# Retention states padded with zeros to all 128 rows, and scores taken two blocks in a row

## The chip, the cores and the metric

The kernel runs on one core of one Trainium2 chip. The metric is the device time of one execution in microseconds (us), 614.69 us before the change as the median of three runs. The chip's engines are named as the profile names them: PE (the matrix engine; PEld is its weight load), DVE (VectorE), ACT (ScalarE), POOL (GpSimd) and SP (SyncE, which here only issues transfers).

## The reference

Retention (a linear attention with a decaying state) over 2 sequences of 768 tokens and 8 heads of 64, and behind it two gated layers on the 1536 tokens. Cut to what matters:

```python
for t in range(S):                                   # S = 768, D = 64, 8 heads, 2 sequences
    state = gamma * state + k[t] v[t]^T              # per head, 64 x 64
    y[t] = scale * q[t] @ state
x = y as (1536 tokens, 512)
x = (x @ w_a) * (x @ w_b) @ w_out                    # 512 -> 1536 -> 512
h = x @ w_in;  out = (h * sigmoid(1.702 h)) @ w_out2 # 512 -> 2048 -> 512
```

## The kernel before

The 1536 tokens are 12 blocks of 128 (`NBLK`), 6 for each sequence (`SEQ`). The retention of block n is worked out in chunks, with all decays moved into scaled copies of q and v, so that the running state is a plain sum in PSUM:

- `att_load(n)` fetches a block in two transfers of 512 KB each on SP's queue: `qv` (q transposed, and v) and `kk` (k transposed, and k). Four buffers of each exist (`RAWBUFS`), so the load of block n+4 waits until block n's have been read: `qv` by `att_q(n)` and `att_v(n)`, `kk` by `att_scores(n)` and `att_kv(n)`. SP issues in program order, so a load that waits holds back all that follow it.
- `att_q(n)` and `att_v(n)` are one POOL instruction each, the scaled q and v of a block.
- `att_scores(n)` (below "sc n"): 8 products k q^T on PE, two heads side by side in the array: head 0 of a pair in rows 0 to 63, head 1 in rows 64 to 127. Then DVE multiplies the 1024 columns by the causal mask (tile `a`). Scores of odd and even blocks have a PSUM tile each.
- `att_kv(n)` ("kv n"): 8 products k^T v, 64 x 64 per head, added to the state in PSUM; ACT copies the state to SBUF. The last block of a sequence needs none.
- `att_av(n)` ("av n" and, except in the first block of a sequence, "st n"): 8 products v^T a and 8 products state^T q into the same PSUM tile. The state products take 64 rows of one head against 64 rows of q, again two heads side by side. ACT and DVE then split the result into a high and a low part, `xh` and `xl`.

Each of these is an fp32 product, for which the profile holds two records: 8 products are x16. All instructions stand in program order by hand (a manual schedule): the loop over n at the end of the kernel writes, for n > 0, sc n+1, then q n+2 and v n+1, kv n, the early work on weights, av n and st n, and the load of block n+4. So PE's order is sc n+1, kv n, av n, st n, sc n+2, and so on.

In between, three 512 KB pieces of the first layer's weights are split into a high and a low part (`w_carry` on ACT; `w_bits`, `w_sign` and `w_add` on DVE, one step per block; `w_parts` on ACT and POOL, tile `wl`), and some more are loaded (`w_dma`, tile `wraw`, on SP's queue too). Behind the loop, `layer(1)` and `layer(2)` are long rows of 128x512 products on PE (`up`, `down`) with the other engines beside them.

Of the kernel before, what the change touches and what calls it, by code (L numbers as in the profile page):

```python
# [7 lines left out]
F32 = mybir.dt.float32  # L8
# [7 lines left out]
P = 128  # L16
B, H, S, D = 2, 8, 768, 64
NP = H // 2
# [6 lines left out]
SEQ = S // P  # L25
# [15 lines left out]
def retention_moe_kernel(  # L41
# [9 lines left out]
    nc = tc.nc  # L51
# [9 lines left out]
    attp = retention.enter_context(tc.tile_pool(name="attp", bufs=2))  # L61
    ps_att = retention.enter_context(tc.tile_pool(name="ps_att", bufs=1, space=PSUM))

    def lo_part(engine, lo, src, hi):
        engine.tensor_tensor(out=lo, in0=src, in1=hi.bitcast(F32), op=ALU.subtract)  # L65
# [8 lines left out]
    gdec = attp.tile([P, SEQ, NP], F32, tag="gdec", name="gdec", bufs=1)  # L74
    qdec = attp.tile([P, SEQ, NP, P], F32, tag="qdec", name="qdec", bufs=1)
    zero = attp.tile([P, P], F32, tag="zero", name="zero", bufs=1)
    x = [xp.tile([P, KD, NT], F32R, tag=t, name=t) for t in ("xh", "xl")]
    qv_t, kk_t, q_t, v_t, a_t, state_t = {}, {}, {}, {}, {}, {}
    kv_t = [None]

    def att_load(n):
        if n >= NBLK:
            return
        qv, kk = (attp.tile([P, 2, DM], F32, tag=t, name=t, bufs=RAWBUFS) for t in ("qv", "kk"))
        if n == 0:
            nc.sync.dma_start(out=qv[:, 0, :], in_=att[n][:, 0, :])
            nc.scalar.dma_start(out=kk[:, 0, :], in_=att[n][:, 1, :])
            nc.scalar.dma_start(out=causal[:, 0, :], in_=cmask[:, 0:P])
            nc.scalar.dma_start(
                out=vdec[:, 0].rearrange("p h o -> p (h o)"), in_=cdec[:, NP * P:NP * P + H]  # L90
            )
            nc.sync.dma_start(out=qv[:, 1, :], in_=att[n][:, 3, :])
            nc.sync.dma_start(out=kk[:, 1, :], in_=att[n][:, 2, :])
            nc.scalar.dma_start(out=qdec[:, 1].rearrange("p a t -> p (a t)"), in_=cdec[:, 0:NP * P])
        else:
            nc.sync.dma_start(out=qv, in_=att[n][:, 0:4:3, :])
            nc.sync.dma_start(out=kk, in_=att[n][:, 1:3, :])  # L97
        qv_t[n], kk_t[n] = qv, kk

    def att_constants():  # L100

        gamma = [1.0 - 2.0 ** (-5.0 - h) for h in range(H)]
        for c in range(1, SEQ):
            for h in range(H):
                nc.gpsimd.memset(vinv[:, c, h, :], gamma[h] ** (-float(P) * c))
        for c in (2, 0, 3, 4, 5):
            for h in range(H):
                rows = slice(64 * (h % 2), 64 * (h % 2) + 64)
                nc.gpsimd.memset(gdec[rows, c, h // 2:h // 2 + 1], gamma[h] ** (float(P) * (c - 1)))
# [6 lines left out]
    def att_qdec(c):  # L116

        if c < SEQ and c != 1:
            for p in range(NP):
                nc.scalar.activation(  # L120
                    out=qdec[:, c, p], in_=qdec[:, 1, p], func=ACTF.Copy, scale=gdec[:, c, p:p + 1]
                )

    def att_q(n):
        if n < NBLK:
            t = attp.tile([P, NP, P], F32, tag="q", name="q", bufs=4)
            (nc.vector if n == 1 else nc.gpsimd).tensor_tensor(  # L127
                out=t, in0=qv_t[n][:, 0, :].rearrange("p (a t) -> p a t", t=P), in1=qdec[:, n % SEQ], op=ALU.mult
            )
            q_t[n] = t  # L130
# [12 lines left out]
    def att_scores(n):  # L143

        if n >= NBLK:
            return
        if n % 2:
            ps = ps_att.tile([P, 2, G], F32, tag="sc", name="ps_sc")
        else:
            ps = ps_a.tile([P, NG, G], F32, tag="set", name="ps_sc")  # L150

        q = qv_t[n][:, 0, :].rearrange("p (a t) -> p a t", t=P) if n == 0 else q_t[n]
        for p in range(NP):
            for h2 in range(2):
                rows = slice(64 * h2, 64 * h2 + 64)
                nc.tensor.matmul(  # L156
                    ps[:, h2, p * P:(p + 1) * P],
                    kk_t[n][rows, 0, p * P:(p + 1) * P],
                    q[rows, p, :],
                    start=True,  # L160
                    stop=True,
                )
        a = attp.tile([P, 2 * NP, P], F32, tag="a", name="a")
        nc.vector.tensor_tensor(
            out=a,
            in0=ps[:, 0:2, :].rearrange("p c (a t) -> p (c a) t", t=P),
            in1=causal.to_broadcast([P, 2 * NP, P]),
            op=ALU.mult,
        )
        a_t[n] = a  # L170

    def att_kv(n):
        c = n % SEQ
        if c == SEQ - 1:
            return
        if c == 0:
            kv_t[0] = ps_att.tile([P, NP, D], F32, tag="kv", name="ps_kv")
        ps = kv_t[0]

        for p in range(NP):  # L180
            for h2 in range(2):
                h = 2 * p + h2
                nc.tensor.matmul(  # L183
                    ps[64 * h2:64 * h2 + 64, p, :],
                    kk_t[n][:, 1, h * D:(h + 1) * D],
                    v_t[n][:, h, :],
                    start=(c == 0 and p == 0),
                    stop=True,
                    skip_group_check=True,
                )  # L190
        t = attp.tile([P, NP, D], F32, tag="state", name="state")
        nc.scalar.copy(t, ps)
        state_t[n + 1] = t

    def att_av(n):
        c = n % SEQ
        ps = ps_att.tile([P, NP, P], F32, tag="av", name="ps_av", bufs=2)
        for p in range(NP):
            for h2 in range(2):
                h = 2 * p + h2  # L200
                nc.tensor.matmul(  # L201
                    ps[64 * h2:64 * h2 + 64, p, :],
                    v_t[n][:, h, :],
                    a_t[n][:, NP * h2 + p, :],
                    start=(p == 0),
                    stop=(c == 0),
                    skip_group_check=True,
                )
        if c > 0:
            for p in range(NP):  # L210
                for h2 in range(2):
                    rows = slice(64 * h2, 64 * h2 + 64)
                    nc.tensor.matmul(  # L213
                        ps[rows, p, :],
                        state_t[n][rows, p, :],
                        q_t[n][rows, p, :],
                        start=False,
                        stop=True,
                        skip_group_check=True,
                    )  # L220
        hi, lo = (t[:, :, n * P:(n + 1) * P] for t in x)
        if n == 0:
            t = attp.tile([P, NP, P], F32, tag="q", name="x0", bufs=4)
            nc.vector.tensor_tensor(out=t, in0=ps, in1=qdec[:, 0], op=ALU.mult)
            ps = t
        nc.scalar.copy(hi, ps)
        lo_part(nc.vector, lo, ps, hi)
# [229 lines left out]
    def warm(ps, n):  # L457

        for _ in range(n):
            nc.tensor.matmul(ps[:, 0, :], zero, zero, start=True, stop=True)  # L460

    with tc.manual_schedule():
        nc.vector.memset(zero, 0.0)
        att_constants()
        for n in range(RAWBUFS):
            att_load(n)
        ps = ps_att.tile([P, NP, P], F32, tag="av", name="ps_warm", bufs=2)
        warm(ps, WARM)
        att_v(0)
        att_vdec([1])  # L470
        nc.vector.tensor_scalar(
            out=causal, in0=causal, scalar1=0.0, scalar2=1.0, op0=ALU.is_gt, op1=ALU.mult
        )
        att_scores(0)
        att_q(1)
        att_qdec(2)
        warm(ps, 12)
        for n in range(NBLK):
            if n > 0:
                att_scores(n + 1)  # L480
            if n == 0:
                att_v(1)
                att_q(2)
                att_vdec(range(2, SEQ))
            else:
                att_q(n + 2)
                att_v(n + 1)
            att_kv(n)
            if n == 0:
                att_qdec(0)  # L490
            if n + 3 < SEQ:
                att_qdec(n + 3)
            w_early(n)
            att_av(n)
            if n == 0:
                att_scores(1)
            if n + RAWBUFS < NBLK:
                att_load(n + RAWBUFS)
            if n in (0, 1, 2, 9):
                w_dma()  # L500
            if n % 3 == 1 and n // 3 < EARLY:
                w_carry(n // 3)
        layer(1)
        layer(2)
# [66 lines left out]
```

## Time and profile before

| what | value |
|---|---|
| runs | 614.69 us median of 3 (614.07 to 614.81) |
| profiled execution | 614.94 us, of which the span from first to last instruction is 613.2 us |
| PE busy | 604.5 us, 99% of the span |
| PEld, DVE, ACT, POOL busy | 502.8, 374.6, 236.9, 149.9 us |
| chain that ended last | PE 97%, of it L340 (`up`) 53% and L377 (`down`) 37% |
| first product of `layer(1)` on that chain | 52.98 us after the span's start |

The retention lies in the first 53 us; the two layers take the rest. A busy PE is not a PE at its peak: between products of different shapes it can stand still inside what the profile calls busy.

### The profile page before, as it was taken

The page shows a single profiled execution, that of the slowest core. Times are in us where ns is not written, and L with a number is a line of the kernel's source. Part 1 is how long each engine was busy: PE and PEld are TensorE (multiplying, and loading weights), DVE is VectorE, ACT ScalarE, POOL GpSimd, SP SyncE. Part 2 cuts the span into 40 slices and gives each one's busy share as a digit, 9 for nine tenths or more (in the row PEclk, how much of TensorE's full clock was granted, in tenths as well). Part 3 has the DMA queues.
Part 4 walks back from the last instruction along what each step waited for, and adds up shares of the span by engine and source line. Part 5 has one row for each costly group of instructions (what it writes and reads, how often), then busy time and mean ns, then how long its engine had stood idle before and what let it go on. Part 6 is the DMA issues. An engine that isn't in the chain of part 4 may idle for free.

```text
span 613.2 us, 7880 instructions
## 1 busy us (share of the span) xinstructions
PE 604.5 (99%) x3198; PEld 502.8 (82%) x3198; DVE 374.6 (61%) x414; ACT 236.9 (39%) x340; POOL 149.9 (24%) x179
## 2 busy tenths in 40 slices
PE   7999999999999999999999999999999999999996
PEld 7888888888888888888888888888888888888885
DVE  1694487882258874156778578825786387826422
ACT  3451455362145530134452365624543155403400
POOL 6692132232023311012332113211212022302000
PEclk9999999999999999999999999999999999999999
DMA  8991133332122322011332011321223111200022
GB/s 304 397 352 38 36 103 104 103 106 66 35 65 73 104 69 69 0 44 60 104 103 81 23 49 54 103 70 35 68 69 103 35 46 57 69 0 1 0 104 103
DMA packets 17043, 52.21 MB, mean 85 GB/s; under 512 B 1776, under 2 KB 1904, under 8 KB 17008
## 3 DMA queue, kind: packets, MB, share of 16 engines
q1 hardware_dynamic: 16432, 51.12, 25.1%
q10 hardware_dynamic: 576, 0.59, 0.3%
q8 instruction: 25, 0.41, 0.3%
q14 instruction: 10, 0.08, 0.0%
HBM read 48.57 MB, written 3.15 MB: 84 GB/s over the span
## 4 chain that ended last, share of the span: by engine, by line
PE 97%; DMA 2%; DVE 0%; POOL 0%; DVEq 0%; SPq 0%; issue 0%; POOLq 0%
PE ps L340 53%; PE ps L377 37%; PE ps_sc L156 2%; PE ps_av L201 2%; PE ps_av L213 2%; DMA qv<-in_att_dram 1%; PE ps_kv L183 1%; DMA kk<-in_att_dram 1%; DVE part L394 0%; POOL q L127 0%; DVEq L567 0%; SPq L97 0%; POOLq L127 0%
## 5 line engine op out<-in xcount | busy, mean ns | idle before, releaser
L65 POOL TENSOR_TENSOR wl<-wt,wh 128x512 fp32r<-128x512 f32 x68 | 116.7, 1719 | 405.7 <-ACT wh L285 375.8
L340 PE MATMUL ps<-xh,wh 128*128 128x512 f32 x480 | 128.9, 389 | 0.0
L340 PE MATMUL ps<-xh,wl 128*128 128x512 f32 x480 | 128.8, 389 | 0.0
L340 PE MATMUL ps<-xl,wh 128*128 128x512 f32 x480 | 128.8, 389 | 0.0
L340 PEld LDWEIGHTS ps<-xh,wl 128*128 128x128 f32 x480 | 90.1, 188 | 18.7
L340 PEld LDWEIGHTS ps<-xh,wh 128*128 128x128 f32 x480 | 90.0, 188 | 18.8 <-issue 0.2
L340 PEld LDWEIGHTS ps<-xl,wh 128*128 128x128 f32 x480 | 90.1, 188 | 18.7
L266 DVE TENSOR_SCALAR wt<-wt 128x512 f32<-128x512 f32 x68 | 65.3, 960 | 53.5 <-ACT wt L260 53.5
L357 ACT CAST gh<-sb 128x1536 fp32r<-128x1536 f32 (+1 forms) x42 | 44.2, 1051 | 112.6 <-DVE sb L356 106.3
L356 DVE TENSOR_TENSOR sb<-ps,sb 128x1536 f32<-128x1536 f32 (+1 forms) x42 | 51.2, 1220 | 48.8 <-ACT sb L440 24.5
L65 DVE TENSOR_TENSOR gl<-sb,gh 128x1536 fp32r<-128x1536 f32 (+1 forms) x42 | 51.5, 1226 | 47.1 <-ACT gh L357 47.1
L394 DVE TENSOR_TENSOR part<-ps,part 128x1536 f32<-128x1536 f32 (+1 forms) x24 | 35.5, 1487 | 48.2 <-PE ps L377 48.2
L273 DVE SCALAR_TENSOR_TENSOR wt<-wraw,wt 128x512 int32<-128x512 int32 x68 | 57.5, 846 | 2.2
L285 ACT CAST wh<-wt 128x512 fp32r<-128x512 f32 x68 | 41.9, 616 | 39.7 <-DVE wt L279 39.7
L377 PE MATMUL ps<-wl,gh 128*128 128x512 f32 x192 | 55.2, 389 | 0.0
L377 PE MATMUL ps<-wh,gh 128*128 128x512 f32 x192 | 55.2, 389 | 0.0
L377 PE MATMUL ps<-wh,gl 128*128 128x512 f32 x192 | 55.2, 389 | 0.0
L279 DVE CUSTOM_DVE_ANT_0 wt<-wraw,wt 128x1024 uint16<-128x1024 uint16 x68 | 50.0, 736 | 6.4
L260 ACT ACTIVATE wt<-wraw 128x512 f32<-128x512 f32 x68 | 45.7, 672 | 1.9 <-POOL wl L65 1.5
L261 ACT ACTIVATE wraw<-wraw 128x512 int32<-128x512 uint32 x68 | 45.3, 667 | 0.0
L440 ACT ACTIVATE sb<-ps 128x1536 f32<-128x1536 f32 (+1 forms) x24 | 23.8, 1029 | 54.1 <-PE ps L340 54.0
L434 ACT COPY sb<-ps 128x1536 f32<-128x1536 f32 x12 | 17.3, 1444 | 66.4 <-PE ps L340 66.4
(47 smaller groups left out, 556.1 us busy)
## 6 DMA issues: line engine op xcount, KB each, us to landing
wraw<-in_w_dram SPq DMA_DIRECT2D x68, 512.0 KB, 3.7
qv<-in_att_dram SPq DMA_DIRECT2D x11, 512.0 KB, 8.3
kk<-in_att_dram SPq DMA_DIRECT2D x11, 512.0 KB, 7.3
out_dram<-part SPq DMA_DIRECT2D x3, 768.0 KB, 3.5
out_dram<-part SPq DMA_DIRECT2D x3, 256.0 KB, 2.1
qv<-in_att_dram SPq DMA_DIRECT2D x2, 256.0 KB, 4.6
kk<-in_att_dram ACTq DMA_DIRECT2D x1, 256.0 KB, 4.2
kk<-in_att_dram SPq DMA_DIRECT2D x1, 256.0 KB, 5.9
```

The costliest lines, as they stand in the source:

```text
L65: engine.tensor_tensor(out=lo, in0=src, in1=hi.bitcast(F32), op=ALU.subtract)
L260: nc.scalar.activation(out=wt[i], in_=high.bitcast(F32), func=ACTF.Abs)
L261: nc.scalar.activation(out=low, in_=low.bitcast(U32), func=ACTF.Copy, scale=2.0 ** -29)
L266: nc.vector.tensor_scalar(out=t, in0=t, scalar1=F64_LOW, scalar2=F64_HIGH, op0=ALU.max, op1=ALU.min)
L273: nc.vector.scalar_tensor_tensor(out=ti, in0=wraw[i][:, :, 1], scalar=-0x40000000, in1=ti, op0=ALU.bitwise_and, op1=ALU.bitwise_or)
L279: nc.vector.tensor_tensor(out=ti, in0=ti, in1=wraw.pop(i)[:, :, 0], op=ALU.add)
L285: nc.scalar.copy(hi, t)
L340: nc.tensor.matmul(ps[:, g, :], l, r, start=(i == 0 and k == 0), stop=(i == 2 and k == max(late or now)), skip_group_check=True,)
L356: nc.vector.tensor_tensor(out=sb[:, c], in0=ps[:, c], in1=sb[:, c], op=ALU.mult)
L357: nc.scalar.copy(gh[:, c], sb[:, c])
L377: nc.tensor.matmul(ps[:, n, :], l, r, start=(f == min(g_t) and i == 0), stop=(f == max(g_t) and i == 2), skip_group_check=True,)
L394: nc.vector.tensor_tensor(out=t[:, c], in0=ps[:, c], in1=t[:, c], op=ALU.add)
```

## The change

Three things change. First, the state gets two fixed tiles of 128 x 4 x 2 x 64, zeroed once on DVE at the start. ACT copies each head's half of the state into its own place, so that the other head's 64 rows stay zero: two copies of 64 partitions each instead of one of 128. Second, the state products take all 128 rows of that tile and of q: the zero rows add nothing, and the product has the shape of the one before it (128 rows, 64 columns). Third, from block 4 on the scores of two blocks stand in a row: at n = 3, 5, 7 and 9 the loop writes sc n+1 and sc n+2, at even n none. For that q is made a block earlier (`att_q(n + 3)` from n = 2 on), q has five buffers and `a` three, and the decays of q are scaled a block earlier.

```diff
+    state = [attp.tile([P, NP, 2, D], F32, tag=f"state{i}", name=f"state{i}", bufs=1) for i in range(2)]
...
-            t = attp.tile([P, NP, P], F32, tag="q", name="q", bufs=4)
+            t = attp.tile([P, NP, P], F32, tag="q", name="q", bufs=5)
...
-        a = attp.tile([P, 2 * NP, P], F32, tag="a", name="a")
+        a = attp.tile([P, 2 * NP, P], F32, tag="a", name="a", bufs=3)
...
-        t = attp.tile([P, NP, D], F32, tag="state", name="state")
-        nc.scalar.copy(t, ps)
-        state_t[n + 1] = t
+        for h2 in range(2):
+            rows = slice(64 * h2, 64 * h2 + 64)
+            nc.scalar.copy(state[(n + 1) % 2][rows, :, h2, :], ps[rows])
...
-                    rows = slice(64 * h2, 64 * h2 + 64)
                     nc.tensor.matmul(
-                        ps[rows, p, :],
-                        state_t[n][rows, p, :],
-                        q_t[n][rows, p, :],
+                        ps[64 * h2:64 * h2 + 64, p, :],
+                        state[n % 2][:, p, h2, :],
+                        q_t[n][:, p, :],
...
         nc.vector.memset(zero, 0.0)
+        for t in state:
+            nc.vector.memset(t, 0.0)
...
         for n in range(NBLK):
-            if n > 0:
+            if n in (1, 2):
                 att_scores(n + 1)
+            elif n % 2:
+                att_scores(n + 1)
+                att_scores(n + 2)
             if n == 0:
                 att_v(1)
                 att_q(2)
                 att_vdec(range(2, SEQ))
             else:
-                att_q(n + 2)
+                if n < 3:
+                    att_q(n + 2)
+                if n > 1:
+                    att_q(n + 3)
                 att_v(n + 1)
             att_kv(n)
             if n == 0:
                 att_qdec(0)
-            if n + 3 < SEQ:
-                att_qdec(n + 3)
+            for c in ((3,), (4, 5))[n] if n < 2 else ():
+                att_qdec(c)
```

On PE, the last stretch of the retention before the change. The names are the program's: q_660 and kk_592 are block 10's, q_710 and kk_643 block 11's; v_662 is block 9's.

```order
L156 MATMUL ps_sc_699<-q_660,kk_592 128x128 x8
L183 MATMUL ps_kv_568<-v_662,kk_550 64x64 x8
L201 MATMUL ps_av_725<-a_658,v_662 64x128 x8
L213 MATMUL ps_av_725<-q_606,state_672 64x128 x8
L156 MATMUL ps_sc_746<-q_710,kk_643 128x128 x8
L183 MATMUL ps_kv_568<-v_712,kk_592 64x64 x8
L201 MATMUL ps_av_772<-a_708,v_712 64x128 x8
L213 MATMUL ps_av_772<-q_660,state_722 64x128 x8
L201 MATMUL ps_av_795<-a_755,v_757 64x128 x8
L213 MATMUL ps_av_795<-q_710,state_767 64x128 x8
```

So sc 11, the last to need loaded data, is followed by kv 10, av 10, st 10, av 11 and st 11. The same stretch after the change, where q_623 and kk_598 are block 10's, q_666 and kk_660 block 11's, and v_668 block 9's:

```order
L158 MATMUL ps_sc_705<-q_623,kk_598 128x128 x8
L158 MATMUL ps_sc_716<-q_666,kk_660 128x128 x8
L185 MATMUL ps_kv_574<-v_668,kk_567 64x64 x8
L203 MATMUL ps_av_740<-a_621,v_668 64x128 x8
L214 MATMUL ps_av_740<-q_570,state1_86 64x128 x8
L185 MATMUL ps_kv_574<-v_727,kk_598 64x64 x8
L203 MATMUL ps_av_776<-a_714,v_727 64x128 x8
L214 MATMUL ps_av_776<-q_623,state0_85 64x128 x8
L203 MATMUL ps_av_799<-a_725,v_761 64x128 x8
L214 MATMUL ps_av_799<-q_666,state1_86 64x128 x8
```

Now kv 9, av 9 and st 9 stand behind sc 11 as well.

On POOL, from q 8 to the last v before the change (q_564 is q 8, v_566 is v 7, then upward by one; wl is the low part of a weight piece):

```order
L127 TENSOR_TENSOR q_564<-qv_502,qdec_83 128x512
L135 TENSOR_TENSOR v_566<-qv_451,vdec_80 128x512
L127 TENSOR_TENSOR q_606<-qv_549,qdec_83 128x512
L135 TENSOR_TENSOR v_608<-qv_502,vdec_80 128x512
L127 TENSOR_TENSOR q_660<-qv_591,qdec_83 128x512
L135 TENSOR_TENSOR v_662<-qv_549,vdec_80 128x512
L65 TENSOR_TENSOR wl_675<-wt_506,wh_674 128x512
L127 TENSOR_TENSOR q_710<-qv_642,qdec_83 128x512
```

And after it, where q_537 is q 8, v_539 v 6, q_570 q 9, and so on:

```order
L129 TENSOR_TENSOR q_537<-qv_508,qdec_83 128x512
L137 TENSOR_TENSOR v_539<-qv_406,vdec_80 128x512
L65 TENSOR_TENSOR wl_542<-wt_355,wh_541 128x512
L129 TENSOR_TENSOR q_570<-qv_566,qdec_83 128x512
L137 TENSOR_TENSOR v_572<-qv_468,vdec_80 128x512
L129 TENSOR_TENSOR q_623<-qv_597,qdec_83 128x512
L137 TENSOR_TENSOR v_625<-qv_508,vdec_80 128x512
L129 TENSOR_TENSOR q_666<-qv_659,qdec_83 128x512
L137 TENSOR_TENSOR v_668<-qv_566,vdec_80 128x512
```

Before, v n stood behind q n+1; now it stands behind q n+2. The order of SP's transfers is the same in both.

## Rows read from the trace of the kernel before

**Rows 1.** Busy time in stretches: PE, PEld, DVE, ACT, POOL, PEclk, DMA share, GB/s.

```profile
20.00:25.00 5.00, 5.00 (x93) 4.41 (x94) 3.34 (x6) 3.80 (x9) 2.75 (x3) 1.00 1.02 390
40.00:45.00 5.00, 5.00 (x92) 4.36 (x90) 4.97 (x6) 3.24 (x6) 4.62 (x5) 1.00 0.99 346
```

**Rows 2.** Chain that ended last, in order of time: start, us, what.

```profile
14.60 1.95 PE ps_sc L156 x16
...
28.27 0.61 PE ps_kv L183 x16
28.89 0.88 PE ps_av L201 x16
...
31.88 1.02 PE ps_av L201 x16
...
46.31 1.02 PE ps_av L213 x16
47.34 1.09 PE ps_sc L156 x16
...
52.98 22.23 PE ps L340 x97
```

**Rows 3.** Groups by line and shape, PEld, 18.2 to 52.9 us.

```profile
L201 PEld LDWEIGHTS ps_av<-a,v 128*64 128x64 f32 x170 | 9.2, 138 | 0.3 <-issue 0.2
L213 PEld LDWEIGHTS ps_av<-q,state 64*64 64x64 f32 x160 | 8.5, 133 | 1.7 <-issue 1.7
```

**Rows 4.** Timeline of SP's queue, issues of loads: start us, us.

```profile
22.62 0.38 SPq L96 DMA_DIRECT2D qv<-in_att_dram  x1
...
26.22 0.38 SPq L96 DMA_DIRECT2D qv<-in_att_dram  x1
...
32.58 0.38 SPq L96 DMA_DIRECT2D qv<-in_att_dram  x1
...
36.10 0.37 SPq L252 DMA_DIRECT2D wraw<-in_w_dram  x1
37.16 0.38 SPq L96 DMA_DIRECT2D qv<-in_att_dram  x1
38.25 0.33 SPq L97 DMA_DIRECT2D kk<-in_att_dram  x1
```

**Rows 5.** Transfers issued at 38.25 (kk) and 50.8 us: KB, us to landing.

```profile
kk<-in_att_dram SPq DMA_DIRECT2D x1, 512.0 KB, 7.3
...
wraw<-in_w_dram SPq DMA_DIRECT2D x1, 512.0 KB, 4.1
```

**Rows 6.** Timeline of POOL: start, us, and in brackets the idle time before.

```profile
26.24 1.55 POOL L127 TENSOR_TENSOR q<-qv,qdec 128x512 f32<-128x512 f32 x1 [0.18 <-DMA qv<-in_att_dram]
...
30.28 1.27 POOL L127 TENSOR_TENSOR q<-qv,qdec 128x512 f32<-128x512 f32 x1 [1.49 <-DMA qv<-in_att_dram]
31.51 1.04 POOL L135 TENSOR_TENSOR v<-qv,vdec 128x512 f32<-128x512 f32 x1
33.16 1.26 POOL L65 TENSOR_TENSOR wl<-wt,wh 128x512 fp32r<-128x512 f32 x1 [0.61 <-ACT wh L285]
34.67 1.27 POOL L127 TENSOR_TENSOR q<-qv,qdec 128x512 f32<-128x512 f32 x1 [0.25 <-DMA qv<-in_att_dram]
...
44.45 1.27 POOL L127 TENSOR_TENSOR q<-qv,qdec 128x512 f32<-128x512 f32 x1 [0.28 <-DMA qv<-in_att_dram]
```

**Rows 7.** Timeline of DVE.

```profile
6.63 0.23 DVE L471 TENSOR_SCALAR causal<-causal 128x128 f32<-128x128 f32 x1 [5.63 <-DMA causal<-in_cmask_dram]
...
22.38 0.41 DVE L266 TENSOR_SCALAR wt<-wt 128x512 f32<-128x512 f32 x1
...
33.19 1.52 DVE L266 TENSOR_SCALAR wt<-wt 128x512 f32<-128x512 f32 x1
```

**Rows 8.** Timeline of ACT.

```profile
17.64 0.37 ACT L192 COPY state<-ps_kv 128x256 f32<-128x256 f32 x1 [1.97 <-PE ps_kv L183]
17.91 1.28 ACT L120 ACTIVATE qdec<-qdec,gdec 128x128 f32<-128x128 f32 x4
20.02 0.59 ACT L226 CAST xh<-ps_av 128x512 fp32r<-128x512 f32 x1 [0.83 <-PE ps_av L213]
```

**Rows 9.** Stretches around PE's wait at 13 us; columns as in Rows 1.

```profile
11.40:14.80 3.40, 1.36 (x18) 1.20 (x20) 0.69 (x1) 3.40 (x13) 2.31 (x4) 1.00 1.04 403
14.80:18.20 3.40, 3.40 (x38) 3.00 (x38) 2.50 (x3) 1.43 (x5) 2.67 (x5) 0.50 1.04 404
```

More of the change, by code (lines that the diff above doesn't have):

```diff
@@ L76, in retention_moe_kernel @@
     zero = attp.tile([P, P], F32, tag="zero", name="zero", bufs=1)
+    state = [attp.tile([P, NP, 2, D], F32, tag=f"state{i}", name=f"state{i}", bufs=1) for i in range(2)]
     x = [xp.tile([P, KD, NT], F32R, tag=t, name=t) for t in ("xh", "xl")]
-    qv_t, kk_t, q_t, v_t, a_t, state_t = {}, {}, {}, {}, {}, {}
+    qv_t, kk_t, q_t, v_t, a_t = {}, {}, {}, {}, {}
     kv_t = [None]
@@ L222, in att_av @@
         if n == 0:
-            t = attp.tile([P, NP, P], F32, tag="q", name="x0", bufs=4)
+            t = attp.tile([P, NP, P], F32, tag="q", name="x0", bufs=5)
             nc.vector.tensor_tensor(out=t, in0=ps, in1=qdec[:, 0], op=ALU.mult)
```

## The prediction

> **What bounds the kernel now.** I read the chain that ended last first. From 14.60 us on it is PE without a break: sc, kv, av, st, block after block, until the first product of `layer(1)` at 52.98 us [rows 2], then products to the end. Nothing in the two layers changes, and the chain runs through PE in them, so whatever moves the start of `layer(1)` moves the whole time by as much. The forecast is about the time 52.98.
>
> Next I read what else is full while PE works. The DMA share is 1.02 in 20 to 25 us and still 0.99 in 40 to 45 us, at 390 and 346 GB/s [rows 1]. A transfer of 512 KB (0.524 MB) thus takes 1.34 us of the DMA early and 1.52 us late. Its delivery can be seen on POOL: q 6, q 7, q 8 and q 11 each started when their `qv` landed, at 26.2, 30.3, 34.7 and 44.45 us [rows 6]. The last `kk`, issued at 38.25, landed 7.3 us later, at 45.55 [rows 4, 5]. So two things run almost abreast: PE, which is never late, and the stream of loads, which ends 1.8 us before sc 11 starts at 47.34 [rows 2]. PE is the bound by that little.
>
> **What PE saves.** av costs 0.88 us behind kv, and 1.02 behind sc [rows 2]: the same 16 records, but another shape in front, so entering a new shape costs 0.14. st (64*64 form) takes 1.02 too, with the same columns. With 128 rows st has the form of av in front of it, and I take it at 0.88: 10 blocks have an st, so 10 x 0.14 = 1.4 us. sc has the same columns as av and takes 1.09: entering it costs 0.21 if its pace is av's, and 0.14 if only the entry counts as elsewhere. Four of the sc now follow another sc, which saves 0.56 to 0.84. kv has half the columns (0.44 by av's pace) and takes 0.61; four of them now follow st and not sc: 0.56 (at 0.14) to 0.68. The sum is 2.5 to 2.9 us; I take 2.7.
>
> Does a product of all 128 rows run at av's pace? In av the weight loads take 138 ns each, and 16 of them, 2.2 us, lie in 0.88 us; in the 64*64 form of st they take 133 ns [rows 2, 3]. So loads overlap in either form, and filling the rows costs nothing. The Trainium skill, page "TensorE: Matmul & The Clock Gate", section "Part 3: Packing small matmuls — row/col tiling", says otherwise: a weight load overlaps running matmuls "only when row_grp differs", and with all 128 rows it never differs. The 128*64 rows of this trace contradict it, and I keep it only as a rival.
>
> **What the rest of the change costs.** The two memsets are 128x512 on DVE, which sits idle for 5.63 us there [rows 7]: nothing, and nothing waits for them before the first state. The state copy becomes two. One takes 0.37 us, and the next ACT instruction starts 0.27 behind it [rows 8], so a second adds 0 (were half the partitions half the time) to 0.37; I take 0.27. In the steady part the copy has av and st of the block, 1.76 us, before kv or st n+1 needs it: hidden. Where av 1 stands, up to 0.4 us may show, but the stream of loads is then the later one. qdec of block 5 moves a block forward, 1.28 us [rows 8]: the cast behind it had 0.83 us of slack, so it comes about 0.7 us later, which only delays xh 1, for which PE asks two blocks later. These I put at zero.
>
> **What pays for it: the order around the loads.** Before, five groups stand behind sc 11: 52.98 - 47.34 = 5.64 us. After, kv 9, av 9 and st 9 stand there too: sc 11 at 0.88 (it follows sc 10), kv 9 0.61, av 0.88, st 0.88, kv 10 0.44, and four times 0.88 makes 7.21. To end at 52.98 as now, sc 11 must start at 45.77, 1.6 us earlier than now. q 11 is ready at 44.45 + 1.27 = 45.72 and its `kk` lands at 45.55. So if the data come exactly when they do now, the change gains nothing: all 2.7 us saved on PE are lost waiting, since PE must have the data one block sooner and there is no faster stream to have them from.
>
> Then the loads themselves come later. The load of `qv` n+4 waits for v n. v n now stands behind q n+2, which waits for the landing of `qv` n+2; before, behind q n+1. I walk POOL (q 1.25, v 1.04, wl 1.26 from start to end [rows 6]) with two cases: DVE's weight steps never hold POOL up, or each time they do, for up to 0.8 us (two steps of 0.41 [rows 7]).
> - q 6 at 26.2, v 4 ends at 28.5 to 29.3. kv 4 started at 28.27 [rows 2]; the same groups stand ahead of it now, less some saving, so PE is ready at about 28 and waits 0.5 to 1.3 us. The load of `qv` 8 goes out then, not at 26.22 [rows 4]. The quickest 512 KB took 4.1 us [rows 5], so it can still land at 34.5 as now.
> - q 7 at 30.3, v 5 ends at 32.6; `qv` 9 follows it, and lands about as now.
> - q 8 at 34.5, v 6 ends at 36.8 to 37.6. PE goes from kv 4 through av 4, st 4, sc 6, sc 7, av 5 and st 5 in 0.44 + 0.88 + 0.88 + 1.09 + 0.88 + 1.02 + 0.88 = 6.07 us, is done at 34.6 to 35.4, and kv 6 waits some 2.2 us. `qv` 10 goes out at 36.8 to 37.6 instead of 32.58, and cannot land before 40.9 to 41.7.
> - wl, q 9, v 7: v 7 ends at 40.3 to 41.1. `qv` 11 goes out 3 to 4 us later than its 37.16. In front of it are `kk` 10 and a weight piece; at 1.3 us each behind `qv` 10 it lands at 44.8 to 45.6, and `kk` 11 at 46.1 to 46.9. At the late pace of 1.52 us, four transfers add 0.8.
> - q 11 ends at 46.1 to 46.9, and sc 11 can start at 46.1 to 47.0. v 9 now stands behind q 11: it ends at 47.2 without a hold and at 48.8 with one. kv 9 starts then, 47.2 to 48.9, and 7.21 - 0.88 = 6.33 us are left.
>
> `layer(1)` would start at 53.5 to 55.2, or 56.0 with slow late transfers. Against 52.98 that is +0.5 to +3.0. I take +2.0: the trace is nearer to the case with holds, since the weight step that takes 0.41 us with POOL idle took 1.52 us while POOL ran wl and q 8 [rows 6, 7]. The Trainium skill, page "SBUF — State Buffer", section "SBUF: two separate sides", calls the port pair of DVE and GpSimd an exclusive lock, where "the other fully blocks"; those two rows agree. By its rule alone the sum would be the upper case, some +2.2.
>
> The sum: 614.94 (profiled execution: span 613.2 and 1.7 around it) + 2.0 = 616.9. The profiled run is 0.25 above the median of the runs, so I forecast **616.7 us**, its own range 615.3 to 618.0.
>
> **The rivals.**
> - *The loads keep their times.* Queue depth may absorb the later issues: the last `kk` took 7.3 us, and 4.1 is possible [rows 5]. Then sc 11 starts at 45.8 and the time is as before, 614.1 to 615.6. Against it: the walk puts the issue of `qv` 10 too late for its landing now.
> - *Faster.* The 2.7 us come through if sc 11 starts at 45.77 - 2.7 = 43.1, so if its `kk` lands 2.5 us sooner than 45.55. From 45.77 on downward each microsecond is one gained. A fuller queue might bring the late 10 us of the stream from 346 back to 390 GB/s, which is 1.1 us, not 2.5, and the sooner issue that this takes is what the new order denies. The whole 2.7 would give 612.0.
> - *PE's clock falls as well.* After PE had worked for 1.36 of 3.40 us, its granted clock was 0.50 (1.2 of 2.4 GHz) in 14.8 to 18.2, and sc took 1.95 us [rows 2, 9]. PE's new waits before kv 4 and kv 6 may bring another such stretch: 1.7 us of lost work, partly under waits. Up to 618.4.
> - *The page's rule on weight loads.* If full-height products kept PE from loading ahead, each of 80 pairs of products in 10 blocks would show its load of 138 ns: 11 us, less 2.7. By the page named above that is 623. The rows of av speak against it.
>
> **How the numbers follow.** A measurement of this kernel can tell about 0.2%, 1.2 us, from no change. The forecast has 0.60, the loads at their times 0.22, the fallen clock 0.09, faster 0.07, the weight-load rule 0.02. The forecast's low end lies within 0.2%, and so may a tenth of its chance: slower 0.65, same 0.28, faster 0.07. The range 614.9 to 618.6 leaves out the faster case, the weight-load rule, the low half of the loads at their times, and little else.
>
> **What would show it.** In the profile after: st at 0.88 us behind av, and sc 5, 7, 9, 11 near 0.9 (PE's saving, right). On the chain that ended last, PE no longer alone, but DMA and POOL before kv 4, kv 6, sc 9, sc 11 or kv 9. `qv` 10 and 11 issued 3 to 5 us later than 32.58 and 37.16. `layer(1)` starting at about 55, and everything behind it as long as now. I am wrong if `kk` 11 lands by 45 us, or if PE waits for nothing between 28 and 48 us.

## The result and the profile after

The changed kernel takes 619.91 us (median of 7 runs, 617.88 to 621.79) against 614.81 for the kernel before, run beside it. The ratio is 1.0073, with a 95% interval of 1.0048 to 1.0097: 4.5 us slower, where 2 were forecast. The profiled execution took 619.91 us, with a span of 618.1. In the table, "kv 2" and "layers" are the starts of kv 2 and of the first product of `layer(1)` in PE's timeline (which shows that product 0.07 us ahead of the chain's 52.98 [rows 2]), and the last column is the profiled execution's time less the start of the layers.

| kernel | kv 2 | layers | kv 2 to layers | profiled | behind |
|---|---|---|---|---|---|
| before | 21.00 | 52.91 | 31.91 | 614.94 | 562.03 |
| changed | 22.59 | 57.87 | 35.28 | 619.91 | 562.04 |

Behind the start of the layers nothing has moved. In these two profiles all 4.96 us stand ahead of it: 1.59 up to kv 2, and 3.37 from there on.

The chain that ended last in the changed kernel, in order of time (start, us, what); before, this stretch was PE alone [rows 2]:

```profile
26.14 1.27 POOL q L129
27.40 1.01 POOL v L137
28.42 0.02 issue
28.43 7.87 DMA qv<-in_att_dram
...
36.44 1.30 POOL q L129
37.74 1.19 POOL v L137
38.93 0.04 issue
38.97 0.82 PE ps_kv L185 x16
39.79 1.71 PE ps_av L203 x16
41.50 2.62 PE ps_sc L158 x32
44.12 0.64 PE ps_kv L185 x16
44.76 0.02 issue
44.77 5.55 DMA kk<-in_att_dram
50.32 0.14 issue
50.46 1.16 PE ps_sc L158 x16
...
57.94 17.23 PE ps L341 x75
```

Read it as a loop. q 6 runs, then v 4; only then does the load of `qv` 8 go out, at 28.43, to land 7.87 us later. q 8, v 6, kv 6, av 6, the scores of blocks 8 and 9, kv 7 follow; only then the load of `kk` 11, which sc 11 waits for. SP's queue for the same loads as in [rows 4] shows how late that is:

```profile
27.05 0.33 SPq L99 DMA_DIRECT2D kk<-in_att_dram  x1
...
28.43 0.38 SPq L98 DMA_DIRECT2D qv<-in_att_dram  x1
...
38.95 0.38 SPq L98 DMA_DIRECT2D qv<-in_att_dram  x1
...
42.85 0.38 SPq L98 DMA_DIRECT2D qv<-in_att_dram  x1
44.77 0.33 SPq L99 DMA_DIRECT2D kk<-in_att_dram  x1
```

These are `kk` 7 and `qv` 8, 10 and 11 and `kk` 11. `qv` 8, 10 and 11 went out 2.2, 6.4 and 5.7 us later than at 26.22, 32.58 and 37.16, and `kk` 11 6.5 us later than at 38.25 [rows 4]. The stream, full before [rows 1], has run thin (columns as there):

```profile
20.00:25.00 5.00, 5.00 (x74) 4.38 (x72) 2.95 (x4) 2.45 (x5) 2.28 (x2) 0.77 0.92 340
40.00:45.00 5.00, 5.00 (x71) 4.55 (x70) 2.42 (x3) 1.43 (x4) 4.33 (x5) 0.72 0.90 286
```

It moved 340 and 286 GB/s, not 390 and 346, and PE's granted clock is 0.77 and 0.72 in these stretches, since it fell to half in 18.9 to 22.3 and in 39.4 to 42.8 us. PE's waits (its timeline; in brackets the idle time before the group and who ended it):

```profile
17.99 1.15 PE L203 MATMUL ps_av<-a,v 128*64 128x128 f32 x16 [2.54 <-DVE a L166]
...
33.86 1.16 PE L158 MATMUL ps_sc<-q,kk 64*128 64x128 f32 x16 [1.18 <-DMA kk<-in_att_dram]
...
38.97 0.82 PE L185 MATMUL ps_kv<-v,kk 128*64 128x64 f32 x16 [2.06 <-POOL v L137]
...
50.46 1.16 PE L158 MATMUL ps_sc<-q,kk 64*128 64x128 f32 x16 [0.67 <-DMA kk<-in_att_dram]
```

### The profile page after: what moved, and what is told of

It reads as the page before. It is cut to its first block, busy times and chain, and to the rows that moved or that the text cites. A ratio compares the mean times of both kernels' runs of the same rounds, so it can differ in the third digit from the quotient of the medians.

```text
span 618.1 us, 7891 instructions
## 1 busy us (share of the span) xinstructions
PE 604.2 (98%) x3198; PEld 505.0 (82%) x3198; DVE 375.0 (61%) x416; ACT 241.2 (39%) x350; POOL 149.8 (24%) x179
## 4 chain that ended last, share of the span: by engine, by line
PE 93%; DMA 3%; ACT 1%; POOL 1%; DVE 1%; ACTq 0%; issue 0%; DVEq 0%; POOLq 0%
PE ps L341 53%; PE ps L378 37%; DMA qv<-in_att_dram 1%; DMA qdec<-in_cdec_dram 1%; PE ps_sc L158 1%; PE ps_av L203 1%; DMA kk<-in_att_dram 1%; PE ps_av L214 1%; ACT qdec L122 1%; PE ps_kv L185 1%; POOL q L129 0%; POOL v L137 0%; DVE xl L65 0%; DVE part L395 0%; ACT L122 0%; DVE a L166 0%
```

## The experiments

Theory A: the order of the loads' readers is to blame, not PE's products. Theory B: the state part is (full-height products, doubled copies). Every kernel ran beside the kernel before; the last two columns are as in the table above. The kernel before had a median of 614.3 to 614.7 us beside most of them and of 616.21 beside 9, 10 and 11, so compare ratios and not only times.

| kernel | us (median) | ratio to before, 95% interval | layers | kv 2 to layers |
|---|---|---|---|---|
| 1 state part alone | 614.99 | 1.0004 (0.9986 to 1.0023) | 52.43 | 30.63 |
| 2 paired scores alone | 620.02 | 1.0073 (1.0045 to 1.0101) | 58.30 | 35.81 |
| 3 changed, 5 load buffers | 615.92 | 1.0013 (0.9996 to 1.0030) | 53.48 | 30.18 |
| 4 changed, v ahead of q | 618.05 | 1.0053 (1.0031 to 1.0074) | 55.63 | 34.64 |
| 5 changed, products on zeros | 619.94 | 1.0071 (1.0046 to 1.0096) | 58.03 | 37.09 |
| 6 state part, sooner first cast | 613.37 | 0.9970 (0.9955 to 0.9986) | 53.91 | 31.24 |
| 7 before, v behind q n+2 | 619.61 | 1.0068 (1.0044 to 1.0093) | 57.83 | 37.37 |
| 8 changed, all mended | 617.10 | 1.0031 (1.0014 to 1.0047) | 55.49 | 34.82 |
| 9 before, fewer loads | 614.78 | 0.9991 (0.9973 to 1.0009) | 54.72 | 31.89 |
| 10 changed, fewer loads | 615.98 | 1.0001 (0.9986 to 1.0015) | 53.80 | 30.83 |
| 11 as 6, 5 load buffers | 613.41 | 0.9962 (0.9949 to 0.9975) | 51.28 | 31.48 |
| 12 as 7, 5 load buffers | 618.21 | 1.0048 (1.0033 to 1.0064) | 56.47 | 32.01 |
| 13 as 12, sooner first cast | 617.99 | 1.0049 (1.0031 to 1.0067) | 56.40 | 36.01 |
| 14 as 3, sooner first cast | 616.01 | 1.0018 (1.0007 to 1.0030) | 53.65 | 30.98 |
| 15 before, sooner first cast | 614.20 | 0.9990 (0.9977 to 1.0002) | 51.90 | 32.22 |

The layers' starts are of one profiled execution each, the medians of many; the profiled execution of 6, at 615.96 us, was the longest of its twelve, and that of 9, at 616.92 us, lies 2.1 above its median. The start of kv 2 (layers less the last column) lies between 19.7 and 24.5 us in these profiles, so a difference of a microsecond in it, from one profile each, need not be the effect of an edit.

**1 and 2: each half by itself.** Kernel 1 has the new state in the old order, kernel 2 the new order with the old state.

```diff
# 1, against the changed kernel
-            if n in (1, 2): ... elif n % 2: ...       # paired scores, q n+3
+            if n > 0:
+                att_scores(n + 1)
...
+                att_q(n + 2)
# 2, against the changed kernel: state copied and multiplied by halves, as before
```

> The changed state tiles, copies and 128-row state products, in the order of the kernel before (scores one block at a time, q and v as before). Theory A (the loss is in the order: v n and kv n free the load buffers a block later, loads go out late, PE waits and its clock falls): no loss here, and 10 state products save 0.14 us each, so 1.4 us faster than before, about 613.3 us. Theory B (the loss is in the state part: full-height products without overlapped weight loads, or the doubled copies): slower than before by 2 us or more.

> The changed order (scores of two blocks in a row, q a block earlier, five q and three a buffers), with the state stored and multiplied as before. Theory A: the whole loss is here, and the 1.4 us of the state products are missing, though part of them hides in PE's waits: 619.5 to 621.5 us. Theory B: 614 us or less.

Theory A held in both as far as the loss goes: kernel 1 lost nothing, though it did not get the 1.4 us either, and kernel 2 has the whole loss. In the chain of kernel 1 one sees PE's saving:

```profile
23.37 0.87 PE ps_av L214 x16
24.24 1.09 PE ps_sc L158 x16
25.33 0.61 PE ps_kv L185 x16
...
52.50 3.63 PE ps L341 x15
```

st takes 0.87 where it took 1.02 [rows 2], and kv 2 to layers shrinks from 31.91 to 30.63. The 1.4 us did not show in the median; in this profile the start took 0.80 us of it, with kv 2 at 21.80. The rule of the Trainium skill ("TensorE: Matmul & The Clock Gate", "Part 3: Packing small matmuls — row/col tiling") that weight loads overlap only between different row groups does not hold for these products: by the prediction's estimate it would have cost kernel 1 some 11 us, and there 16 weight loads of 137 ns each lie within the 0.87 us of an st.

**3 and 4: loads sooner, v sooner.**

```diff
# 3 (and the tile pool of the layers opened after the retention, for room)
-        qv, kk = (attp.tile(..., bufs=RAWBUFS) for t in ("qv", "kk"))
+        qv, kk = (attp.tile(..., bufs=5) for t in ("qv", "kk"))
# 4
+                att_v(n + 1)
                 if n > 1:
                     att_q(n + 3)
-                att_v(n + 1)
```

> The changed kernel with five instead of four buffers for each load of a block (the tile pool of the layers is opened after the retention to make room), so that the load of block n+4 waits for block n-1's readers. Theory A: loads go out as early as before or earlier, the stream stays full, the last one lands at 44 to 46 us instead of 50.4, and the layers start at 52.5 to 54: 614 to 616 us. Theory B, or if waits on loads were not the cause: 619 to 620 us as the changed kernel.

> The changed kernel with v n+1 written ahead of q n+3 on GpSimd, so that v is no longer behind a q that waits for its load; the kk load still waits for a kv that stands behind two scores. Theory A: the kv 4 and kv 6 waits shrink and part of the loss comes back, 615.5 to 618 us. Theory B: 619 to 620 us.

A fifth buffer takes the layers back from 57.87 to 53.48 us: 4.4 of the 4.96 us are the late loads (by the ratios, 0.60% of the 0.73%). What is left, 0.57 us in these profiles, is not a wait for the last loads. `kk` 11 landed at about its old time (45.5 us against 45.55), and PE did not wait ahead of sc 11. From kv 2 on kernel 3 is 1.73 us shorter than the kernel before, so part of PE's saving came through; but its kv 2 came 2.30 us later. The waits that PE has left are on GpSimd, for q 9 ahead of sc 9 and for v 7 ahead of kv 7:

```profile
39.11 1.16 PE L157 MATMUL ps_sc<-q,kk 64*128 64x128 f32 x16 [0.19 <-POOL q L128]
40.56 0.69 PE L184 MATMUL ps_kv<-v,kk 128*64 128x64 f32 x16 [0.29 <-POOL v L136]
```

Kernel 4 gave back less than half; there sc 9 waited 2.74 us for q 9, which now stood behind v 7 and a weight piece.

**5: the clock.** Products on zeros where PE waited, to keep it busy.

```diff
+            if n == 6:
+                att_warm(6, 7)
             att_kv(n)
+            if n == 1:
+                att_warm(1, 8)
```

> The changed kernel with products on zeros added where PE waited: 8 ahead of av 1 and 7 ahead of kv 6, into the PSUM tile that the av of that block overwrites. If the fallen clock is a cause of its own, the granted clock stays at 1.00 over the two stretches that showed 0.50 (18.9 to 22.3 and 39.4 to 42.8 us), st 1 and sc 3 take 0.87 and 1.09 us instead of 1.71 and 1.81, and av 6, sc 8 and sc 9 likewise: 1.4 us come back at the first and up to 1.7 at the second, so 616.5 to 618.5 us. If the clock only falls where PE has time anyway, the waits grow by as much and the time stays at 619 to 620.5.

The stretches at half clock are gone from these two places (PEclk, the third last column), and the time is the same:

```profile
18.90:22.30 3.40, 3.40 (x68) 3.11 (x66) 1.84 (x3) 2.26 (x5) 0.22 (x2) 1.00 1.04 407
39.40:42.80 3.40, 3.40 (x68) 3.28 (x70) 2.83 (x3) 1.27 (x3) 1.74 (x2) 1.00 0.97 332
```

The layers still start at 58.03. kv 2 came at 20.94, 1.65 us sooner than in the changed kernel, and none of it reached the layers: PE waited longer instead, 0.54, 1.22 and 1.97 us ahead of kv 4, 6 and 8, each for its v, and its clock fell behind the last of them, at 46.2. So the clock is not a cause of its own at 18.9 and 39.4; what its fall at 46.2 cost was not separated.

**6, 11 and 15: the start, and versions that beat both kernels.** One move: the decays of block 3 behind the first cast.

```diff
-            if n + 3 < SEQ:
+            if 0 < n and n + 3 < SEQ:
                 att_qdec(n + 3)
...
             att_av(n)
             if n == 0:
+                att_qdec(3)
                 att_scores(1)
```

> The state part alone, as in the run of the state part in the old order, with the scaling of q's decays for block 3 moved behind the cast of block 0, so that the first split and with it the mask of block 1 come 1.2 us sooner. If the wait ahead of av 1 (2.6 us there, on the mask behind a split that waits for ACT) hides what the state products save, av 1 starts at 15.5 to 16.5 instead of 17.5 and the layers at 51 to 51.8 instead of 52.5, until the loads bound it: 612.8 to 613.8 us, faster than before. If the start is not on the path, 615 us as without it.

> The state part in the old order with the decays of block 3 behind the first cast (the run that was 0.3% faster than the kernel before), and five load buffers, so that loads go out a block earlier. If the stream of loads is now what holds PE in the last blocks, the last kk lands up to 1 us sooner and the layers start at 50.5 to 51.5: 612 to 613.3 us. If PE is the bound, the same 613.4 as without the buffers.

> The kernel before with that one move at the start and nothing else. If the gain of the state part with the move (0.3%) came from the state products (1.3 us from kv 2 on), this run is within 0.2% of the kernel before, 613.8 to 615; if it came from the start, it is 0.2% or more faster, 612.5 to 613.4.

The state part with this move is 0.3% faster than the kernel before, with five buffers 0.4%; between the two (613.37 and 613.41 us) there is no difference that these runs can tell. The move alone gives 0.1% with an interval that reaches 1.0002. So it looks as if most of the gain is the state products, but that is not shown: the intervals of 6 and 15 overlap, and the state products without the move (kernel 1) gained nothing. The state products are the half of the change that needs no data sooner. The sooner start does not show in the profile of 6 (kv 2 at 22.67; st 1 and sc 3 took 1.63 and 1.94 us there), but it does in those of 11 and 15 (19.80 and 19.68).

**7, 12 and 13: v late by itself.**

```diff
# 7, against the kernel before (q five buffers, decays a block earlier)
-                att_q(n + 2)
+                if n < 3:
+                    att_q(n + 2)
+                if n > 1:
+                    att_q(n + 3)
                 att_v(n + 1)
# 12: and bufs=5 for qv and kk, as in 3.   13: and the move of 6.
```

> The kernel before (its state products, scores one block at a time) with one edit: q is made a block earlier on GpSimd, so that v n stands behind q n+2, as after the change (five q buffers, decays of q a block earlier). Theory A1 (v alone frees the qv buffers late and starves the stream): most of the loss, 616.5 to 619 us, loads of qv 10 and 11 issued 3 us or more later. Theory A2 (it takes the paired scores ahead of kv too, which hold back the kk loads): 614 to 616 us.

> The kernel before with v n behind q n+2 on GpSimd (the one edit that cost 5 us by itself) and five load buffers, so that the load of qv n+4 waits for v n-1 and no longer closes a loop from one landing to the next issue. Theory L (the loss is the loop: landing of qv n+2, q n+2, v n, issue of qv n+4, its landing, every two blocks): 614 to 615.5 us, as before, though every v is as late on GpSimd as without the buffers. Rival (v late on GpSimd makes PE wait for kv by itself, whatever the loads do): 617 to 620 us.

> The run with v late and five load buffers, and the scaling of block 3's decays moved behind the first cast, so that the mask of block 1 comes some 1.2 us sooner and PE's wait ahead of av 1 shrinks. If its 3.5 us were lost at the start alone (stretch from kv 2 on 32.0 us, as before), kv 2 starts at 20 to 22.5 us instead of 24.5 and the time is 613.5 to 616. If v late costs in some way that the stretch from kv 2 on doesn't show, it stays at 618.

One edit on GpSimd, with no change to PE's order, costs 4 to 5 us (4.2 by the ratio, 4.92 at the start of the layers). The loads of `qv` 10 and 11 went out at 37.19 and 41.11, 4.6 and 4.0 us later than before [rows 4]. Some of PE's waits in kernel 7, ahead of kv 6, 7 and 9:

```profile
37.22 0.69 PE L183 MATMUL ps_kv<-v,kk 128*64 128x64 f32 x16 [1.26 <-POOL v L135]
...
41.14 0.69 PE L183 MATMUL ps_kv<-v,kk 128*64 128x64 f32 x16 [1.26 <-POOL v L135]
...
49.67 0.69 PE L183 MATMUL ps_kv<-v,kk 128*64 128x64 f32 x16 [1.25 <-POOL v L135]
```

Here my loop theory got its own test, and fell for the larger part. In 12 the loads land as in the kernel before (`kk` 11 at 44.75 us against 45.55 [rows 4, 5]), and yet 3.5 of the 4.9 us stay. Kernel 12 hides why: it lost 3.5 us ahead of kv 2, and from there PE never waited. Kernel 13 begins 4.1 us sooner and ends at the same place, 56.40. Its longest waits behind kv 2:

```profile
37.13 0.69 PE L182 MATMUL ps_kv<-v,kk 128*64 128x64 f32 x16 [1.24 <-POOL v L134]
...
41.03 0.69 PE L182 MATMUL ps_kv<-v,kk 128*64 128x64 f32 x16 [1.25 <-POOL v L134]
```

The second is kv 7. The kernel before started it at 37.53, and from kv 7 on both need 15.4 us. On GpSimd, v 7 stands behind q 9, behind a weight piece, behind q 8 and v 6, and q 8 cannot start before its load has landed:

```profile
34.80 1.27 POOL L126 TENSOR_TENSOR q<-qv,qdec 128x512 f32<-128x512 f32 x1 [2.17 <-DMA qv<-in_att_dram]
36.03 1.04 POOL L134 TENSOR_TENSOR v<-qv,vdec 128x512 f32<-128x512 f32 x1
37.03 1.27 POOL L64 TENSOR_TENSOR wl<-wt,wh 128x512 fp32r<-128x512 f32 x1
38.27 1.71 POOL L126 TENSOR_TENSOR q<-qv,qdec 128x512 f32<-128x512 f32 x1
39.94 1.04 POOL L134 TENSOR_TENSOR v<-qv,vdec 128x512 f32<-128x512 f32 x1
```

So with v late alone, 3.5 us are this pin (kv n tied to the landing of block n+2) and 1.4 us (57.83 less 56.4) the loads that go out late. With the scores paired, PE has more done by then (from kv 7 on it needs 12.9 us in kernel 3 and not 15.4) and the pin weighs less: there the late loads are 4.4 of 4.96.

**8, 9, 10 and 14: is the stream the bound?** Kernel 8 puts everything sooner; 9 and 10 take 2 MB out of the stream; 14 is kernel 3 with the move of 6.

```diff
# 8: 5 buffers, att_v(n + 1) ahead of att_q(n + 3), the move of 6, and
             elif n % 2:
+                att_kv(n)
                 att_scores(n + 1)
                 att_scores(n + 2)
# 9 and 10: k as kv takes it is loaded for n < 4 alone
-            nc.sync.dma_start(out=kk, in_=att[n][:, 1:3, :])
+            nc.sync.dma_start(out=kk, in_=att[n][:, 1:2, :])
```

> The changed kernel with all that holds its loads back undone: five load buffers, v n+1 ahead of q n+3 on GpSimd, kv n ahead of the paired scores on PE (no more changes of shape than behind them), and the decays of q for block 3 behind the first cast. Theory A: the stream stays full and the last kk lands at 44.5 to 45.5 us; behind sc 11 still lie about 7.2 us of products, so the layers start at 52 to 53: 613.5 to 615 us, no slower than before but hardly faster, since the stream and not PE is the bound.

> The kernel before with 2 MB less in the stream of loads: k as kv takes it is loaded for blocks 0 to 3 alone, and kv of a later block n takes block n mod 4's, so the later blocks' k is left out of the result; all instructions on the engines stay. PE is the bound in the kernel before, so theory A expects little: 612.5 to 614.5 us, the layers from 51.5 to 53.

> The changed kernel with the same loads left out (k of blocks 4 to 11 as kv takes it). Theory A (the new order needs data that the stream has not yet brought, and loses only by that): with loads ahead of PE the change turns from 5 us slower into 1.5 to 2.7 us faster than the kernel before with the same loads left out, 610.5 to 612.5 us. If the loss were in the order on GpSimd and PE whatever the loads do, it would stay 2 us or more slower than that kernel.

> The whole change with five load buffers and the same move at the start. The stretch from kv 2 on took 30.2 us with five buffers; if the start then is as short as in the fastest run of the state part (kv 2 at 20 to 21), the layers begin at 50.2 to 51.5: 612.3 to 613.6 us, faster than the kernel before. If PE's saving is eaten by waits for the loads once the start is sooner, the stretch grows to 31.5 and the time is 613.5 to 615.

Kernel 8 missed: its last `kk` landed at 44.23, yet the layers start at 55.49. kv 7 now stood ahead of the paired scores and waited 2.41 us for v 7, which stood behind q 8 and the weight piece, with two scores queued behind it; PE's clock then fell at 39.8. Taking a wait out of one place put it in another. Kernel 9 is as the kernel before, as expected, though its 614.78 us lie 0.3 above the range. Kernel 10 lies between the theories: 1.2 us over kernel 9, not 5 and not under it. Its chain says why fewer bytes do not help enough:

```profile
25.17 1.27 POOL q L135
26.44 1.01 POOL v L143
27.45 0.02 issue
27.47 5.74 DMA qv<-in_att_dram
...
33.34 1.29 POOL q L135
34.63 1.00 POOL v L143
```

The loop of landing, q, v, issue and landing takes 8.2 us for two blocks, 5.7 of them from issue to landing although the stream has room (DMA share 0.86, 279 GB/s in 27.5 to 33.2 us).

Kernel 14 missed its better case too. Its kv 2 came at 22.67, 0.63 us sooner than in kernel 3 but not sooner than in the kernel before, and its layers start 0.17 later than in kernel 3. A still sooner start would not have helped it, for its chain does not run over PE's start: `qv` 8 landed at 33.90, and q 8, v 6, a weight piece and q 9 follow on GpSimd until PE can start sc 9, from where on it does not wait:

```profile
36.57 0.69 PE L184 MATMUL ps_kv<-v,kk 128*64 128x64 f32 x16 [1.02 <-POOL v L136]
...
39.67 1.16 PE L157 MATMUL ps_sc<-q,kk 64*128 64x128 f32 x16 [0.45 <-POOL q L128]
```

So no version of the whole change was faster than the kernel before. Kernels 3 and 14 stay 0.1 to 0.2% slower, where the interval of 3 reaches 0.9996.

## Why the prediction was wrong, and where it was right

The direction and the mechanism were right: the change makes PE ask for data a block sooner and sends the loads out later, PE waits, and the layers start later by exactly what the time grows. The size was wrong, +2.0 forecast against 4.5 to 5.1.

- *PE's saving*: as forecast. st 0.87 for 1.02; kv 2 to layers 1.28 us shorter in kernel 1, for 9 of the 10 st. The wait ahead of kv 6 was as forecast too, 2.06 us for some 2.2; ahead of kv 4, where 0.5 to 1.3 were forecast, there was none, since PE came to it later than forecast.
- *Break-even*: the count was right, the place was not. From sc 11 on I counted 7.21 us; it was 57.87 - 50.46 = 7.41. With the loads near their old times (kernel 3), the layers start 0.57 us later than before, so the change gains nothing, as said. But sc 11 did not wait for data there: q 9 and v 7 on GpSimd did the holding, behind q 8, v 6, a weight piece and the landing of `qv` 8 at 33.8.
- *The landing of the loads*: the step that failed, in two places. First, "it can still land at 34.5 as now": `qv` 8 went out at 28.43, as the walk had it, but landed at 36.3, 7.87 us later, with `kk` 7 and a weight piece issued 1.4 and 1.0 us ahead of it. I had left it 6 us, from the quickest transfer of 4.1 [rows 5], though the same load had taken 8.3 us in the kernel before, from 26.22 [rows 4] until q 8 could start [rows 6]. Second, "it lands at 44.8 to 45.6, and `kk` 11 at 46.1 to 46.9": `kk` 11 landed at 50.3, and sc 11 started at 50.46 instead of 46.1 to 47.0. I walked only the issue of `qv`, and put each `kk` 1.3 us behind it as in a full stream. But `kk` 11 waits for kv 7, and kv 7 now stands behind sc 8 and sc 9, and these behind kv 6, which waited for v 6: `kk` 11 went out at 44.77, 1.92 us behind `qv` 11, and took 5.55 us to land. This is the term that was short, by 3.4 to 4.2 us. Not every `kk` waits for a kv: `kk` 7 went out at 27.05, when sc 5, the second score of its pair, had ended, and 0.6 us ahead of the end of kv 3.
- *Start*: I allowed 0.4 us; kv 2 came 1.59 later in the profile. Of that, 1.41 us are st 1 and sc 3 at the fallen clock, 1.71 and 1.81 us for 1.02 and 1.09; in kernel 5, where PE was kept busy ahead of av 1, they are gone. The first split took DVE 1.47 us while GpSimd's q 3 ran (0.69 before, where it began ahead of q 3), which the Trainium skill ("SBUF — State Buffer", "SBUF: two separate sides") would call the shared port pair's exclusive lock. But kernel 9, with the old order at the start, shows 1.62 as well, so this is no sure effect of the change, and kernels 5, 12 and 13 show that a start sooner by 1.65 or 4 us is not passed on once the loads pin PE.
- *Clock*: the rival did happen, at 39.4, but kernel 5, without it there, is as slow.
- *v 9's hold on GpSimd*, the term on which I put the most between my ends, did not matter: v 9 ended at 51.02, and kv 9 followed sc 11 at once.

Open: what part of the start's 1.59 us belongs to the change; and the last 0.6 us that five buffers leave, of which no run took q 9 and the weight piece on GpSimd apart.

## What to carry to other kernels

When a producer's instruction is moved ahead in an in-order queue, ask what then stands behind it, and which buffer that one frees: here v, which needed nothing new, was put behind a q that waits for a load, and with it the next loads. Walk every load of the loop by its last reader, not the one at hand, since a load into a stream that has run thin costs its time from issue to landing (5.55 us for `kk` 11) and not the pace of a full one (1.3 to 1.5 us). Where an engine is the bound by a small margin (1.6 us here), a saving on it can be lost whole, as here, if it needs the next bound's data sooner; the half that needs none (the state products) can be taken by itself.

## What the runs showed of the hardware

A granted clock that has fallen can stay down over much work. In kernel 12 it was 0.50 for over 10 us, in which PE was busy for 8.98 of 10.30 us, with one wait of 1.32 us inside (columns as in [rows 9]):

```profile
14.50:24.80 10.30, 8.98 (x86) 7.68 (x88) 5.15 (x6) 5.58 (x16) 6.68 (x8) 0.50 1.03 400
```

In the kernel before, with no wait in that place, it was 0.50 from 14.80 to 18.20 [rows 9] and 1.00 behind it:

```profile
18.20:21.60 3.40, 3.40 (x64) 2.94 (x62) 1.42 (x3) 2.18 (x6) 2.59 (x3) 1.00 1.03 395
```

Products of 128x64 weights over all 128 rows and of 64x64 weights side by side run at the same pace here: in st of the kernel before (64x64) and of kernel 1 (128x64), a pair of records starts 0.11 us after the pair before. 16 records of 128x64 take 0.87 us behind their own shape. Only the change of shape costs, 0.14 to 0.2 us each time.
